# Token mixing of the second and third pair of batches: the first product as seven block products, with sums on GpSimd and shared results in PSUM

## The chip, the cores and the metric

The kernel runs on one core of a Trainium2 chip. The time is the device time of one execution in microseconds. Before the change it is 770.59 us, the median of three runs (770.36 to 770.64).

## What is computed

An attention block without softmax, with 8 batches of 8 heads, 576 rows and a head width of 64, is followed by a mixer. The attention's output, normalised per head, is laid out as x with 576 rows and 512 columns per batch.

```python
kv = np.einsum('bhsd,bhse->bhde', k, v)
out = np.einsum('bhsd,bhde->bhse', q, kv)
rms = np.sqrt(np.mean(out * out, axis=-1, keepdims=True) + 1e-06)
x = out / rms * g_norm                      # then (B, S, H*D)
...
xt = x.transpose(0, 2, 1)
h = np.maximum(xt @ w_tok1, 0.0) @ w_tok2   # 576 -> 256 -> 576
u = x + h.transpose(0, 2, 1)
h2 = np.maximum(u @ w_ch1, 0.0) @ w_ch2     # 512 -> 1536 -> 512
return u + h2
```

The change concerns `xt @ w_tok1`, the first product of token mixing.

## The kernel before

**Tiles and stages.** Batches are handled in four pairs. X of a pair lies in five tiles: four of 128 partitions x 2 x 512 (X[pair, 0] and X[pair, 1] hold the first 512 rows of the pair's first batch, the "side" 0; X[pair, 2] and X[pair, 3] those of side 1), and one of 128 x 512 with the last 64 rows of both batches (X[pair, 4]). Attention of pair p + 1 is interleaved with token mixing of pair p on every engine. When all pairs are done, a channel stage computes the rest from rows that were written to the output in memory and from transposed blocks; it takes most of the time (about 185 us to the end). It is written with seven block products in place of eight already, and so is not touched.

**Order.** The order of work on each engine is written out by hand. `play` (L1317) reads strings of step names and calls each step; every instruction is kept in program order on its engine. The strings `middle` (L1385, mixing of pair 0 and attention of pair 1) and `steady` (L1391, pairs 1 and 2 of the mixing) are the ones that change. A name with "-" belongs to the attention or mixing of the pair before in time, a digit n runs n steps of the weight rounding (clamp L202, shift L206, an addition L211 on DVE, and two scaling activations, L181 and L186 or L196 and L199, on ACT).

**Names.** For a group c of X: a{c} is the attention's product on PE into the PSUM pools o or kv; g{c}{h} multiplies by the gain on DVE (L494); q{c}{h} squares on ACT (L498); t{c}{h} sums the squares on DVE (L522); m, r and i form the inverse of the root mean square (L527 on DVE, L532 on ACT, L536 to L541 on DVE). Then X is scaled: s{c}{t} on ACT (eight activations, L557), d{c}{t} on DVE (L566), p{c}{t} on POOL (L570). kv{s}{h} is the product of k and v on PE and e{s}{h} its copy out on ACT. x{u}{half} are transposes of X on DVE into the unused part of the tile of the second channel weight, and b{u}{half} the DMAs that put them away. f{n} fetches a block of the channel weights, l, lq and lr load k, v and q.

**Token mixing** (`token_mixing`, L598). h{s}{t} (`tok1`, L601) adds four products of 128 x 128 by 128 x 512 into a PSUM bank for side s and half t of the 256 hidden columns; PSUM pool h has four banks. hr (`tok1_rem`, L608) adds the last 64 rows and writes h1 with four Relu activations. z{i} (`seed`, L619) copies a tile of x into a bank ahead of time, so that the second product lands on top of it. u{i} (`tok2`, L625) is the second product: without a seed its result is added to x by DVE, with a seed it is copied back by ACT; every second u, and u8, issues DMAs to the output from the POOL queue. Before the change the seeds are 2, 4 and 6, and the order around the change is: kv00, kv01, u8 and a3 of the neighbouring pairs, h00, h01, a0, h10, h11, hr, a1.

The helpers have one line for all their uses: `tensor_add` L127, `relu` L130, `copy` L133, `matmul` L136, `dma` L124.

Of the kernel before, what the change touches and what calls it, by code (L numbers as in the profile page):

```python
# [11 lines left out]
F32 = mybir.dt.float32  # L12
# [3 lines left out]
ALU = mybir.AluOpType  # L16
# [4 lines left out]
def kernel(  # L21
# [32 lines left out]
    nc = tc.nc  # L54
    P = 128
    B, S, DM = k.shape
# [4 lines left out]
    J, JJ, HF, Q = 4, 5, 64, 32  # L61
    LO = P * J
    assert D == 64 and DM == 512 and S == LO + HF and B % 2 == 0
    NC, NF, NTOK = DM // P, DCH // P, DTOK // P
# [6 lines left out]
    NU = B + 1  # L71
    NG = 1 + B // 2
    T = 2 * P
    assert B // 2 == 4
    EPS = 1e-6
    TOP = (2.0 - 2.0 ** -3 - 2.0 ** -23) * 2.0 ** -96

    def pool(name, bufs, side="left", stack=ctx, **kw):
# [9 lines left out]
    hp_ = pool("hp", 2, "right", right)  # L88
# [7 lines left out]
    ps = {n: pool(f"ps_{n}", b, "left", psums, space=bass.MemoryType.PSUM)  # L96
          for n, b in (("o", 2), ("kv", 2), ("h", 4))}
# [4 lines left out]
    w_tok1 = [tokw.tile([P, 2, DTOK], F32, name=f"w_tok1{i}") for i in range(J // 2)]  # L102
    w_tok1r = tokw.tile([P, DTOK], F32, name="w_tok1r")
# [3 lines left out]
    w_ch2 = w2p.tile([P, 2, NS, 2, DH], F32, name="w_ch2")  # L107
    k_in = [inp.tile([P, JJ, DM], F32, name=f"k_in{i}") for i in range(2)]
# [6 lines left out]
    def do(f, *a, **kw):  # L115
        return lambda: f(*a, **kw)
# [6 lines left out]
    def dma(o, i, engine=nc.sync):  # L123
        keep(engine.dma_start(o, i))  # L124

    def tensor_add(o, a, b, op=ALU.add, engine=nc.vector):
        keep(engine.tensor_tensor(out=o, in0=a, in1=b, op=op))  # L127

    def relu(o, a):
        keep(nc.scalar.activation(o, a, AF.Relu))  # L130

    def copy(o, a):
        keep(nc.scalar.copy(o, a))  # L133

    def matmul(*a, **kw):
        keep(nc.tensor.matmul(*a, **kw))  # L136
# [120 lines left out]
    def get_ch2(f):  # L257

        def loads(raw):
            t = raw.rearrange("p (f n) w -> p f n w", f=2)  # L260
            rows = words(moe_w_ch2)[ts(f, 2 * P)].rearrange("(f p) n w -> f p n w", f=2)
            return [(t[:, i], rows[i]) for i in range(2)]

        dst = w_ch2[:, 2 * f // NS, ds(2 * f % NS, 2)]
        return block(2 * DM, loads, dst.rearrange("p f h n -> p (f h n)"), True)
# [115 lines left out]
    X = {}  # L381

    def x_of(pair, i):

        return X[pair, i // 2][:, i % 2]
# [209 lines left out]
        return steps  # L595


    def token_mixing(pair, seeds, aside=()):  # L598
        h1, acc = {}, {}

        def tok1(side, t, js=range(J)):  # L601
            if js[0] == 0:
                acc[side, t] = ps["h"].tile([P, DM], F32, name="ps_h", tag="h")
            for j in js:
                matmul(acc[side, t], lhsT=w_tok1[j // 2][:, j % 2, ts(t, P)],
                                 rhs=x_of(pair, side * J + j), start=(j == 0), stop=False)

        def tok1_rem():  # L608
            for t in range(NTOK):
                for side in range(2):  # L610
                    r = ds(side * HF, HF)
                    matmul(acc[side, t], lhsT=w_tok1r[r, ts(t, P)],
                                     rhs=x_of(pair, 8)[r], start=False, stop=True)
            for side in range(2):
                h1[side] = hp_.tile([P, NTOK, DM], F32, name="h1", tag="h1")
                for t in range(NTOK):
                    relu(h1[side][:, t], acc[side, t])

        def seed(i):  # L619


            acc[i] = ps["h"].tile([P, DM], F32, name="ps_u", tag="h")
            copy(acc[i], x_of(pair, i))

        def tok2(i):  # L625
            if i not in seeds:
                n = "o" if i in aside else "h"
                acc[i] = ps[n].tile([P, DM], F32, name="ps_u", tag=n)
            first = i not in seeds
            if i < 8:  # L630
                for t in range(NTOK):
                    matmul(acc[i], lhsT=w_tok2[:, t, ts(i % J, P)], rhs=h1[i // J][:, t],
                           start=(first and t == 0), stop=(t == NTOK - 1), skip_group_check=True)
            else:
                for t in range(NTOK):
                    for side in range(2):
                        matmul(acc[i][ds(side * HF, HF)], lhsT=w_tok2[:, t, LO:],
                               rhs=h1[side][:, t],
                               start=(first and t == 0), stop=(t == NTOK - 1), skip_group_check=True)
            x = x_of(pair, i)  # L640
            if first:
                tensor_add(x, acc[i], x)
            else:
                copy(x, acc[i])
            if i == 8:
                dma(u_rest[ts(pair, P)], x, nc.gpsimd)
                for side in range(2):
                    dma(out[2 * pair + side, LO:], x[ds(side * HF, HF)], nc.gpsimd)
            elif i % 2 == 1:
                dma(  # L650
                    u_rows(2 * pair + i // J)[ds((i % J - 1) * P, 2 * P)]
                    .rearrange("(t p) e -> p t e", p=P), X[pair, i // 2], nc.gpsimd)

        steps = {f"h{s}{t}": do(tok1, s, t) for s in range(2) for t in range(NTOK)}
        steps |= {f"h{s}{t}{j}": do(tok1, s, t, (j,)) for s in range(2) for t in range(NTOK) for j in range(J)}
        steps |= {f"z{i}": do(seed, i) for i in seeds}
        return steps | {"hr": tok1_rem} | {f"u{i}": do(tok2, i) for i in range(9)}


    xg, xt, uT = {}, {}, {}  # L660
# [656 lines left out]
    def play(lines, after={}, **stages):  # L1317

        for name in " ".join(lines).split():
            if name.isdigit():
                for _ in range(int(name)):
                    next(stages["rounding"], lambda: None)()
            elif name[0] == "-":
                stages["before"][name[1:]]()
            else:
                next(stages[s][name] for s in ("attention", "mixing", "more")
                     if name in stages.get(s, ()))()
# [3 lines left out]
    tok2 = [get_tok2(t) for t in range(NTOK)]  # L1333
    first_rows = [get_tok1_half(j) for j in range(2)]
    channel = ([get_ch1(c, f) for f in range(2) for c in range(NC)]
               + [get_ch2(f) for f in range(NF // 2)])
    dma(g_row, bass.AP(tensor=g_norm.tensor, offset=g_norm.offset, ap=[[0, 1], list(g_norm.ap[0])]), nc.gpsimd)
    load(0)
    first_rows[0][0]()
# [32 lines left out]
    def spread_g():  # L1372
# [12 lines left out]
    middle = [  # L1385
        "h100 h110 h101 h111 w31 w22 w23 w24", "kv00 e00 -lq1 w32 w33 w34",
        "h102 h112 h103 h113 w41 w42 w43 w44", "kv01 e01", "hr l0 z2",
        "a0 q00 g01 q01 g00 t00 t01", "u0 f0", "u1 z4", "u2", "a1 q10 g11 q11 g10",
        "kv10 kv11 e10 e11 t10 t11 m0 r0 lq0", "u3 z6 i0 d00 s01 d11 f1", "u4 l1", "a2 q20 g21 q21 g20",
        "a4 q40 t20 g41 q41 t21 g40 lr0 lr1", "u5 s10 t40 t41 m2 r2 f2 1", "u6 1 i2 p20 p21 x00", "u7 1 1"]  # L1390
    steady = [[  # L1391
        "kv00 kv01 e00 e01 -d40 f3", "-u8 -a3 -q30 -g31 -q31 -g30 -t30 -t31 -m3 -r3 -lq1",
        "h00 -i3 -d31 -s30 l0 b00 1 1", "h01 f4 x01 1", "a0 q00 g01 q01 g00", "h10 t00 t01 b01 x10 1",
        "h11 1 x11 1", "hr z2 f5 f6", "a1 q10 g11 q11 g10 lq0", "kv10 kv11 e10 e11 t10 t11 m0 r0", "u0 i0 1",
        "u1 z4 d00 s01 l1", "u2", "a2 q20 g21 q21 g20", "a4 q40 t20 g41 q41 t21 g40 lr0 lr1", "u3 z6 d11 1",
        "u4 s10 t40 t41 m2 r2 1 f7", "u5 i2 d20 p21 1 1", "u6 1 f8", "u7 1 1 b10 b11"], [
        "kv00 kv01 e00 e01 -d40 f9", "-u8 -a3 -q30 -g31 -q31 -g30 -t30 -t31 -m3 -r3 -lq1",
        "h00 -i3 -d31 -s30 x20 1", "h01 x21 1", "a0 q00 g01 q01 g00", "h10 t00 t01 1 1", "h11 f10 1 1", "hr z2",
        "a1 q10 g11 q11 g10", "kv10 kv11 e10 e11 t10 t11 m0 r0", "u0 f11 i0 1", "u1 z4 d00 s01", "u2",
        "a2 q20 g21 q21 g20", "a4 q40 t20 g41 q41 t21 g40", "u3 z6 d11 1", "u4 s10 t40 t41 m2 r2 1",  # L1400
        "u5 i2 d20 p21 1", "u6 1 f12 b20 b21", "u7 1", "a3 q30 g31 q31 g30", "u8 t30 t31 m3 r3 f13"]]

    attentions = [attention(0, ((0,), (1,), (2,), (3,), (4,)))]
    attentions += [attention(p, ((0, 1), (2, 4), (3,))) for p in range(1, B // 2)]

    mixings = [token_mixing(p, (2, 4, 6)) for p in range(B // 2 - 1)]
    mixings.append(token_mixing(B // 2 - 1, range(2, 9), (0, 1)))
    more = {f"w{n}{k}": f for n, b in enumerate(first_rows[:1] + tok1[1:] + tok2 + first_rows[1:]) for k, f in enumerate(b)}
    more |= {f"f{n}": b[0] for n, b in enumerate(channel)}
# [11 lines left out]

    more |= {f"j{n}": do(keep_warm, n) for n in (4, 5, 21)}
    more["gs"] = spread_g
    more |= {f"zk{side}{half}": do(spread_k, side, half) for side in range(2) for half in range(2)}
    more |= {f"zz{side}": do(zero_rows, side) for side in range(2)}
    play(start, attention=attentions[0], mixing=mixings[0], more=more)
    play(middle, attention=attentions[1], mixing=mixings[0], before=attentions[0],
         more=more, rounding=rounding)
    for n in range(1, B // 2 - 1):
        play(steady[n - 1], attention=attentions[n + 1], mixing=mixings[n], before=attentions[n] | {"u8": mixings[n - 1]["u8"]},  # L1430
             more=more, rounding=rounding)


# [113 lines left out]
```

## Time and profile before

| | |
|---|---|
| median of the runs | 770.59 us |
| span of the profiled execution | 768.4 us |
| PE busy | 762.0 us, 4694 matmul records |
| DVE busy | 644.5 us |
| ACT busy | 279.5 us |
| POOL busy | 112.8 us |
| first product of token mixing, all four pairs | 128 records of 128 x 512 and 32 of the last rows |
| DMA, mean rate | 245 GB/s |

The span runs from the first to the last instruction of one profiled execution; the run's own time lies 2.2 us above it. The profile lists, for each engine, how long it was busy, and the timeline gives each instruction's start, its length, and in brackets the idle time before it and what ended that. A matmul of single precision leaves two records. PE's records have modelled ends, so starts are used here and not lengths. A group of records that is merged in one line carries the start of its first and the time to the end of its last.

### The profile page before, as it was taken

The numbers are of one execution on the slowest core, as the hardware profiler recorded it, in microseconds if no ns is written. First come the engines' busy times: TensorE is split into PE (matmuls) and PEld (weight loads), VectorE is DVE, ScalarE is ACT, GpSimd is POOL, SyncE is SP. The second block draws the span as 40 slices with busy tenths as digits, with TensorE's granted clock in tenths as the row PEclk, the third lists the DMA queues.
The fourth block names the chain that finished last, engine by engine and source line by source line (L and its number), as shares of the span: only waits on it lengthen the run. The fifth ranks groups of instructions, "written<-read, shape, count | busy, mean of one in ns | idle before, by whom it ended". The sixth has DMA issues, their size and how long they took to land.

```text
span 768.4 us, 12735 instructions
## 1 busy us (share of the span) xinstructions
PE 762.0 (99%) x4694; PEld 614.3 (80%) x4694; DVE 644.5 (84%) x956; ACT 279.5 (36%) x563; POOL 112.8 (15%) x125
## 2 busy tenths in 40 slices
PE   9999999999999999999999999999999999999997
PEld 8655555446888888888888888888888888888887
DVE  4868886997757779899968989997898997798996
ACT  3656666773210332512234241123352213325221
POOL 1003030204410000002240002042000227000204
PEclk9999999999999999999999999999999999999999
DMA  9999997599798795599998578999659889855679
GB/s 353 374 374 371 367 373 279 177 332 333 245 290 319 288 284 169 168 275 214 224 228 250 152 221 219 262 187 265 193 154 293 160 227 209 200 153 155 153 192 119
DMA packets 137981, 188.28 MB, mean 245 GB/s; under 512 B 48704, under 2 KB 95808, under 8 KB 135872
## 3 DMA queue, kind: packets, MB, share of 16 engines
q1 hardware_dynamic: 102240, 168.72, 69.1%
q0 software_dynamic: 34848, 18.36, 16.1%
q8 instruction: 38, 0.62, 0.3%
q10 hardware_dynamic: 832, 0.39, 0.2%
q14 instruction: 23, 0.19, 0.1%
HBM read 138.28 MB, written 49.15 MB: 244 GB/s over the span
## 4 chain that ended last, share of the span: by engine, by line
PE 96%; DMA 2%; DVE 1%; SPq 0%; ACT 0%; issue 0%; DVEq 0%
PE ps_d L136 28%; PE ps_b L136 19%; PE ps_a L136 19%; PE ps_u L136 8%; PE ps_h L136 8%; PE ps_v L136 5%; PE ps_c L136 3%; PE ps_w L136 2%; PE ps_kv L136 2%; PE ps_o L136 2%; DMA raw<-in_moe_w_tok_dram 1%; DMA v_in<-in_k_dram 1%; PE ps_r L136 0%; DVE x L494 0%; DVE ms L522 0%; DVE w_tok L211 0%
## 5 line engine op out<-in xcount | busy, mean ns | idle before, releaser
L136 PE MATMUL ps_d<-ui,w 128*128 128x256 f32 x504 | 118.6, 379 | 0.0
L136 PEld LDWEIGHTS ps_d<-ui,w 128*128 128x128 f32 x504 | 95.8, 190 | 13.0
L133 ACT COPY ps_d<-ps_a 128x768 f32<-128x768 f32 (+1 forms) x56 | 32.0, 572 | 199.9 <-PE ps_a L136 196.9
L127 DVE TENSOR_TENSOR v<-v,v 128x1536 f32<-128x1536 f32 (+2 forms) x70 | 103.2, 1482 | 0.3
L136 PE MATMUL ps_b<-sv,w 128*128 128x256 f32 x324 | 78.9, 379 | 0.0
L136 PE MATMUL ps_a<-v,w 128*128 128x256 f32 x324 | 78.7, 379 | 0.0
L1266 POOL DMA_DIRECT2D out_dram<-us x24 | 26.8, 1835 | 291.8 <-ACT p L133 286.5
L136 PEld LDWEIGHTS ps_b<-sv,w 128*128 128x128 f32 x324 | 61.2, 190 | 8.9 <-issue 0.6
L136 PEld LDWEIGHTS ps_a<-v,w 128*128 128x128 f32 x324 | 61.6, 190 | 8.4
L136 PE MATMUL ps_u<-h,w_tok 128*128 128x512 f32 (+1 forms) x160 | 64.7, 599 | 0.0
L136 PE MATMUL ps_d<-v,w 128*128 128x256 f32 x258 | 62.7, 379 | 0.0
L130 ACT ACTIVATE v<-v 128x768 f32<-128x768 f32 (+1 forms) x54 | 42.6, 822 | 55.1 <-DVE v L127 52.3
L136 PE MATMUL ps_h<-x,w_tok 128*128 128x512 f32 x128 | 57.6, 600 | 0.7 <-DVE w_tok L211 0.6
L1266 POOL DMA_DIRECT2D out_dram<-r x40 | 41.3, 1926 | 102.0 <-ACT p L133 80.3
L136 PE MATMUL ps_d<-sv,w 128*128 128x256 f32 x228 | 55.4, 379 | 0.0
L136 PEld LDWEIGHTS ps_d<-v,w 128*128 128x128 f32 x258 | 48.9, 190 | 6.6
L136 PEld LDWEIGHTS ps_u<-h,w_tok 128*128 128x128 f32 (+1 forms) x160 | 25.6, 179 | 31.1 <-issue 26.7
L136 PEld LDWEIGHTS ps_d<-sv,w 128*128 128x128 f32 x228 | 43.3, 190 | 5.9
L136 PE MATMUL ps_a<-uT,w 128*128 128x256 f32 x192 | 46.7, 379 | 0.0
L136 PEld LDWEIGHTS ps_h<-x,w_tok 128*128 128x128 f32 x128 | 23.5, 190 | 28.3 <-issue 24.4
L136 PE MATMUL ps_b<-ui,w 128*128 128x256 f32 x168 | 40.8, 379 | 0.0
L136 PEld LDWEIGHTS ps_a<-uT,w 128*128 128x128 f32 x192 | 36.5, 190 | 5.0
(178 smaller groups left out, 1297.7 us busy)
## 6 DMA issues: line engine op xcount, KB each, us to landing
w<-parts SPq DMA_DIRECT2D x168, 384.0 KB
w<-parts SPq DMA_DIRECT2D x56, 192.0 KB
uT<-blocks SPq DMA_DIRECT2D x36, 256.0 KB
k_in<-in_k_dram SPq DMA_DIRECT2D x8, 1024.0 KB
v_in<-in_v_dram SPq DMA_DIRECT2D x8, 1024.0 KB
qT<-in_q_dram SPq DMA_DIRECT2D x8, 1024.0 KB
out_dram<-x POOLq DMA_DIRECT2D x16, 512.0 KB, 6.9
raw<-in_moe_w_ch_dram SPq DMA_DIRECT2D x8, 768.0 KB
```

The source lines that it names most:

```text
L127: keep(engine.tensor_tensor(out=o, in0=a, in1=b, op=op))
L130: keep(nc.scalar.activation(o, a, AF.Relu))
L133: keep(nc.scalar.copy(o, a))
L136: keep(nc.tensor.matmul(*a, **kw))
L1266: keep(nc.gpsimd.dma_start(to, t()[ds(b * Q, Q), at].rearrange("p n l j -> p n (l j)"), accum_op=ALU.add))
```

## The change

In the second and third pair (`fast = (1, 2)`), the eight block products of the first product (two halves of the hidden columns, two halves of the rows, two sides; each block product is two matmuls) are replaced by seven, on sums of blocks:

- Four sums of blocks of `w_tok1` (`mix_tok1`, y1 to y4 in `middle`) are formed once on POOL, 128 x 256 each, and kept in a part of the second channel weight's tile that is filled late.
- Four sums of blocks of X (`t_sum`: y1, y2, T1 or T2, and y4 per pair) are formed on POOL, two subtractions of 128 x 512 each. T stands in the line of u5 or u4, in the phase before; y1 and y2 follow u8 on the queue; y4 follows p6.
- The products p1 to p7 run in the order p3, p7, p1, a0, p6, p2, p5, p4 on four banks. Bank a gets p1; ACT copies it to bank e in PSUM, and p6 and p5 are added there; p2 is added to bank a, p7 and p4 share bank d, p3 has bank y. ACT copies out the state of d after p7, and that of e after p6 and after p5.
- hr (`p_rem`) adds the last rows, three additions on DVE join the banks with what was copied out, and three Relu activations write h1.
- Seeds 3 and 5 are added in these pairs (z3, z5), so that u3 and u5 are copied back by ACT.
- The DMAs of u8's rows become a step v8 (`put_rest`) that stands behind y1 and y2 on the POOL queue. The transposes x11 move from h11's place to u0's, and the order of the last blocks of the second channel weight changes.

```diff
+    def tok_sum(n):
+        return weight_room[1].rearrange("p s (g n) -> p (s g) n", n=2 * P)[:, n - 1].rearrange(
+            "p (j n) -> p j n", j=2)
+    def mix_tok1(n):
+        a = lambda m, k: w_tok1[k][:, :, ts(m, P)]
+        x, y, op = {1: (a(1, 0), a(1, 1), ALU.add), 2: (tok_sum(1), a(0, 0), ALU.subtract),
+                    3: (a(0, 0), a(1, 0), ALU.subtract), 4: (a(0, 1), tok_sum(2), ALU.subtract)}[n]
+        tensor_add(tok_sum(n), x, y, op, nc.gpsimd)
...
+        b_block = {11: 2, 12: 0, 21: 3, 22: 1}
+        def t_sum(n):
+            b = lambda name: X[pair, b_block[name]]
+            if n < 3:
+                h1[n - 1] = hp_.tile([P, NTOK, DM], F32, name="h1", tag="h1")
+            txs[n] = h1[0] if n == 1 else h1[1] if n != 3 else spare(pair, 0)
+            x = b({1: 12, 4: 21}.get(n, 22))
+            y = b({1: 11, 3: 12}[n]) if n % 2 else h1[n // 4]
+            for j in range(2):
+                tensor_add(txs[n][:, j], x[:, j], y[:, j], ALU.subtract, nc.gpsimd)
+        def product(name, lhs, rhs, start):
+            if start:
+                bank[name] = ps["h"].tile([P, DM], F32, name="ps_h", tag="h")
+            for j in range(2):
+                matmul(bank[name], lhsT=lhs[:, j], rhs=rhs[:, j], start=(start and j == 0),
+                       stop=False, skip_group_check=True)
+        def p3():
+            product("y", tok_sum(4), x_block(22), True)
+        def p7():
+            product("d", tok_sum(3), txs[3], True)
+            copy(spare(pair, 1)[:, 0], bank["d"])
+        def p1():
+            product("a", a_block(0, 0), x_block(11), True)
+            bank["e"] = ps["h"].tile([P, DM], F32, name="ps_h", tag="h")
+            copy(bank["e"], bank["a"])
+        def p6():
+            product("e", tok_sum(2), txs[2], False)
+            copy(spare(pair, 1)[:, 1], bank["e"])
+        def p2():
+            product("a", a_block(0, 1), x_block(21), False)
+        def p5():
+            product("e", tok_sum(1), txs[1], False)
+            copy(h1[0][:, 0], bank["e"])
+        def p4():
+            product("d", a_block(1, 1), txs[4], False)
+        def p_rem():
...
+            tensor_add(h1[0][:, 0], bank["y"], h1[0][:, 0])
+            tensor_add(h1[0][:, 1], bank["e"], spare(pair, 1)[:, 0])
+            tensor_add(h1[1][:, 1], bank["d"], spare(pair, 1)[:, 1])
+            relu(h1[0], h1[0])
+            relu(h1[1][:, 0], bank["a"])
+            relu(h1[1][:, 1], h1[1][:, 1])
...
-               + [get_ch2(f) for f in range(NF // 2)])
+               + [get_ch2(f) for f in (0, 1, 2, 4, 5, 3)])
...
     steady = [[
-        "kv00 kv01 e00 e01 -d40 f3", "-u8 -a3 -q30 -g31 -q31 -g30 -t30 -t31 -m3 -r3 -lq1",
-        "h00 -i3 -d31 -s30 l0 b00 1 1", "h01 f4 x01 1", "a0 q00 g01 q01 g00", "h10 t00 t01 b01 x10 1",
-        "h11 1 x11 1", "hr z2 f5 f6", "a1 q10 g11 q11 g10 lq0", "kv10 kv11 e10 e11 t10 t11 m0 r0", "u0 i0 1",
...
+        "kv00 kv01 e00 e01 -d40 f3", "-u8 y1 y2 -v8 -a3 -q30 -g31 -q31 -g30 -t30 -t31 -m3 -r3 -lq1",
+        "p3 -i3 -d31 -s30 l0 b00", "p7 1 1", "p1 f4 x01 1", "a0 q00 g01 q01 g00", "p6 y4 t00 t01 b01", "p2 x10 1", "p5 1", "p4 1",
+        "hr z2 z3 f5 f6", "a1 q10 g11 q11 g10 lq0", "kv10 kv11 e10 e11 t10 t11 m0 r0", "u0 x11 i0 1",
...
-    mixings = [token_mixing(p, (2, 4, 6)) for p in range(B // 2 - 1)]
+    mixings = [token_mixing(p, (2, 3, 4, 5, 6) if p in fast else (2, 4, 6)) for p in range(B // 2 - 1)]
```

The third pair's string changes likewise, with one difference that the prediction uses: there "p7 x20 1" and "p1 x21 1" carry one rounding step each, where the second pair has "p7 1 1".

## The prediction

> **What bounds the kernel now.** I read the page first (busy shares, the clock row, the chain that ended last), then the list of waits, then the timeline around the two phases that change, PE first, then ACT, then DVE and POOL.
>
> ```profile
> PE 762.0 (99%) x4694; PEld 614.3 (80%) x4694; DVE 644.5 (84%) x956; ACT 279.5 (36%) x563; POOL 112.8 (15%) x125
> ...
> PEclk9999999999999999999999999999999999999999
> ...
> PE 96%; DMA 2%; DVE 1%; SPq 0%; ACT 0%; issue 0%; DVEq 0%
> ```
>
> PE is busy for 762.0 of 768.4 us, at full clock in every slice, and is 96% of the chain. The list of waits gives PE only two semaphore waits, 1.7 us together, both in the first stage. So a matmul taken out shortens the run by its length, and any new wait of PE lengthens it by the wait: no idle time stands ready to swallow it. This is the second pair's phase on PE:
>
> ```profile
> 69.06 1.16 PE L136 MATMUL ps_o<-kvp,qT 64*64 64x64 f32 x64
> 70.15 7.13 PE L136 MATMUL ps_h<-x,w_tok 128*128 128x512 f32 x16
> 77.21 1.16 PE L136 MATMUL ps_o<-kvp,qT 64*64 64x64 f32 x64
> 78.30 7.13 PE L136 MATMUL ps_h<-x,w_tok 128*128 128x512 f32 x16
> ```
>
> Step a3 starts at 69.06, h00 and h01 at 70.15, a0 at 77.21, h10 and h11 at 78.30. Each matmul leaves two records, so 16 records are 8 matmuls: 77.21 - 70.15 = 7.06 us, 0.88 us each. The third pair shows the same from 111.84.
>
> **What goes.** Sixteen matmuls per pair become fourteen (seven products of two); the instruction lists of the two kernels confirm it. Four fewer at 0.88: **-3.53 us**, all on the path.
>
> **What comes: a wait of PE for ACT.** PE's new order is p3, p7, p1, a0, p6, p2, p5, p4. p6 adds onto bank e, which must first hold p1's result, and an ACT copy brings it there. PE takes its steps in order, so while p6 waits, p2, p5, p4, hr, a1 and all behind them wait too. With p3 at 70.15, PE is ready for p6 at 70.15 + 3 x 1.77 + 1.09 (a0) = 76.54. When is the copy done? ACT is in order as well, and the instruction lists put ahead of it: s30 (eight scalings of X[1,3]), the copy of bank d after p7, and in this pair one rounding step of two activations. ACT in the trace of before:
>
> ```profile
> 75.40 0.21 ACT L532 ACTIVATE root<-ms 128x16 f32<-128x16 f32 x1 [1.33 <-DVE ms L527]
> 76.64 2.02 ACT L557 ACTIVATE x<-x,inv 128x64 f32<-128x64 f32 x8 [1.02 <-DVE inv L541]
> 78.57 0.89 ACT L181 ACTIVATE w_ch<-raw 128x768 f32<-128x768 f32 x1
> 79.37 0.90 ACT L186 ACTIVATE raw<-raw 128x768 uint32<-128x768 uint32 x1
> 80.17 0.57 ACT L498 ACTIVATE sq<-ps_o 128x512 f32<-128x512 f32 x1
> ```
>
> s30 waits until 76.64 for statistics that begin with a3 on PE, which the change leaves where it was. ACT is free of s30 at 78.57; the two rounding activations take 80.17 - 78.57 = 1.60. A copy of 512 columns I take at 0.58 (the rows of ps_u<-x and x<-ps_u have 602 and 576 ns). So p6 cannot start before 78.57 + 0.58 + 1.60 + 0.58 = 81.33: **4.8 us of stall**, where before h10 needed nothing from ACT. In the third pair no rounding stands between:
>
> ```profile
> 111.84 7.13 PE L136 MATMUL ps_h<-x,w_tok 128*128 128x512 f32 x16
> ...
> 116.34 2.02 ACT L557 ACTIVATE x<-x,inv 128x64 f32<-128x64 f32 x8 [1.03 <-DVE inv L541]
> ...
> 118.90 1.16 PE L136 MATMUL ps_o<-kvp,qT 64*64 64x64 f32 x64
> ```
>
> PE is ready at 111.84 + 5.30 + 1.09 = 118.23; ACT at 116.34 + 1.93 + 2 x 0.58 = 119.43: **1.2 us**. These two are floors, as they assume that DVE's statistics come no later than before. Floor of the sum: 4.8 + 1.2 - 3.53 = +2.5 us.
>
> **GpSimd beside DVE.** Each fast pair gets eight POOL subtractions of 512 columns, two (T) before s30's statistics, four (y1, y2) during them, two (y4) behind p6. A POOL operation of 512 has 1245 ns in the mean with waits, and 0.92 to 1.03 without; one of 384 with two full inputs 0.95 to 1.1. I take 1.15. DVE is without idle time from 66.3 to 75.2 (and from 104.8 to 115.1) except for waits on ACT's square root, so what delays DVE delays s30. And POOL does delay it:
>
> ```profile
> 105.97 1.55 POOL L570 TENSOR_TENSOR x<-x,inv 128x512 f32<-128x512 f32 x1
> ...
> 106.52 1.42 DVE L202 TENSOR_SCALAR w_ch<-w_ch 128x768 f32<-128x768 f32 x1
> ...
> 107.98 0.56 DVE L206 TENSOR_SCALAR w_ch<-w_ch 128x768 uint32<-128x768 uint32 x1
> ```
>
> L202 alone takes 0.55; beside a POOL operation that ended at 107.52 it took 1.42, that is, 0.42 past that end. At 147.78 an L211 took 2.08 where its five likes take 1.22 in the mean, again until a POOL operation had ended. If every DVE operation with two inputs in SBUF, the 128x16 ones too, takes turns like this with T, y1 and y2, the inverse that s30 waits for comes 2.7 us later in the second pair: T runs from 65.65 (after s10 and a DMA issue) to 68.4 with L202 between its halves, and holds the two 128x16 operations behind L202 (+1.25); d40 meets y1's first half (some +1.0 more) and L527 the end of y2 (+0.45). In the third pair it is 2.8: ACT's added copy for u3 puts T beside the next inverse (+1.2), p21 comes between L202 and L206 (+0.6), y2 holds L527 (+1.0). If none of this reaches the chain, it is 0. No row shows the small ones beside POOL. I take 1.7 and 1.4, between the ends, nearer the upper in the second pair since T lies right on a 128x768 operation there. Stalls: 6.5 and 2.6 us. The Trainium skill's page "SBUF — State Buffer" (Who interferes with whom) speaks against moving sums to GpSimd here: it calls the shared port pair an exclusive lock for DVE operations in a 2-port mode or with two SBUF inputs. By that rule the delays would be the full 2.7 and 2.8, and the sum below 2.4 us higher.
>
> **The clock.** PE is never idle for long in the trace until its end. There its last matmul ends at 762.25 + 1.50 = 763.75:
>
> ```profile
> 1.07:4.00 2.93, 2.93 (x13) 1.00 0.78 232
> 4.00:6.40 2.40, 2.40 (x13) 1.00 1.00 410
> 6.60:8.40 1.80, 1.80 (x18) 1.00 1.00 386
> ...
> 767.00:767.60 0.60, 0.00 (x0) 1.00 0.00 0
> 767.70:768.40 0.70, 0.00 (x0) 0.50 0.03 12
> ```
>
> The columns are PE's busy time with its records, the clock, DMA. The clock halves some 3.95 us after the last matmul. At the start the same 128-column matmuls pass at 0.18 us a record until about 6.5, then at 0.10: PE, busy from 1.07, took some 5.4 us to get full speed (though the clock's column says 1.00 there). A stall of 6.5 us outlasts 3.95, so the clock should fall in the second pair; 5.4 us at half speed lose up to 2.7 us, none if it holds. I take 2.0. The page "TensorE: Matmul & The Clock Gate" (Part 1) gives windows of about 3.4 us free running, both ways. By it a resumed PE loses 1.7 to 3.4 us, and the sum below would be +7.3 to +9.0.
>
> **What costs nothing.** p7 and p1 wait for POOL's T and p21: done by about 71.3, needed at 71.9 and 73.7. y2 ends near 77.7 and 117.6: before p6 can start anyway, though with only 0.6 to spare in the third pair if ACT were early. p5 needs bank e copied out (0.58), covered by p2's 1.77; p4 needs y4 (2.3), covered by p2 and p5 (3.5). After hr DVE has three additions (0.69) and ACT a Relu of 1024 columns (1.05) ahead of u0; a1 and kv on PE cover 3.57 us, so u0 is late only if DVE is over 1 us late. ACT gains about 4.5 us per pair and sheds no bound; DVE gains three additions and loses two. The seeds z3 and z5 fill banks two products ahead of use. y1, y2 now stand on POOL's queue ahead of the last rows' three DMAs (1.7 us of issue), T ahead of p21 and of one DMA: the rows are read only in later stages, and p21 is needed by p1 alone. The four weight sums (128x256) run in the first pair's phase where POOL idles; the transposes x11 and the order of the last weight blocks only change place on DVE, ahead of a stage that starts after all of them.
>
> **The sum.** 6.5 + 2.6 + 2.0 - 3.53 = +7.6: span 768.4 -> 776.0, and with the 2.2 us by which the median (770.59) lies above the profiled span, **778.2 us**. A difference under 0.2% (1.5 us) can't be told from none.
>
> **The rivals.**
> - *Floor* (0.25): POOL doesn't hold the chain, the clock holds. +2.5 gives 773.1; up to 776. For it: no row shows a small DVE operation held. Against it: DVE has no slack.
> - *Both stalls in full* (0.13): 7.5 + 4.0 and the clock falls twice (2 x 2.7): +13.4, 784.0; from about 781. The third pair's stall would have to pass 3.95 us.
> - *The inputs come in time* (0.06), the other side: bank e is filled before a0 ends, in both pairs, and seven products simply replace eight: -3.53, 767.1. It decides as soon as the two stalls together stay under 3.53 us. For it: ACT is only 36% busy, and DVE sheds additions before the third pair. Against it: s30's place in ACT's list.
> - *Both even out* (0.04): within 0.2%.
> - That the product count doesn't fall is excluded by the instruction lists.
>
> The forecast (stalls with part of the turns, clock falls once; 776 to 781) has 0.52. The range 773.0 to 782.5 takes in the floor and part of the full stalls; it leaves out the two faster or equal cases and the far end, some 0.18. Faster 0.06, same 0.04, slower 0.90.
>
> **What would show it.** The waits of the changed kernel should have PE waiting for ACT's ps_h<-ps_h copy, once over 4.8 us and once over 1.2; ACT's timeline s30, then the copies; the granted clock below 1 in the stretch after the first stall; DVE's operations at 66 to 76 us longer beside POOL. The forecast is wrong if ACT's copy of bank e starts before s30 is done, if a3's statistics finish earlier, or if the clock stays at 1.00 through a stall of over 5 us (then 2 us less).

## The result, and the profile after

The changed kernel takes 796.88 us (median of 4 runs, 794.81 to 797.65) against 770.54 us for the kernel before: a ratio of 1.0339, 95% interval 1.0326 to 1.0351. The prediction was 778.2 us with a range to 782.5, so the side was right and the size far off: +26.3 us instead of +7.6. The profiled execution took 796.38 us, with a span of 794.5.

The page of the changed kernel, in the lines that answer to those of before: the span, the busy row, the clock in 40 slices of 19.9 us, the chain.

```profile
span 794.5 us, 12774 instructions
...
PE 763.3 (96%) x4686; PEld 613.6 (77%) x4686; DVE 661.9 (83%) x958; ACT 286.6 (36%) x577; POOL 135.7 (17%) x145
...
PEclk9999698799999999999999999999999999999999
...
PE 78%; DVE 5%; ACT 5%; SPq 1%; issue 1%; DMA 0%; ACTq 0%; DVEq 0%
```

PE is busy about as long as before (763.3 us against 762.0) and the span is 26 us longer: PE is waiting. The clock falls in two places, slice 5 and slices 7 and 8, which are the second and third pair. The list of PE's waits (total, times, longest):

```profile
PE ps_h L137 <- ACT ps_h L134: 21.8, 2, 11.6
PE ps_u L137 <- ACT h L131: 2.1, 1, 2.1
```

The first is the wait that was predicted, PE for the copy of bank a into bank e on ACT, once in each pair, but of 11.6 and 10.2 us instead of 6.5 and 2.6. The second, 2.1 us in the last pair, was not predicted at all. The second pair's phase on PE (start, length, and in brackets the idle time before):

```profile
70.09 1.98 PE L137 MATMUL ps_h<-x,w_ch 128*128 128x512 f32 x4
71.91 1.88 PE L137 MATMUL ps_h<-w_ch 128*128 128x512 f32 x4
73.63 1.88 PE L137 MATMUL ps_h<-x,w_tok 128*128 128x512 f32 x4
75.44 1.16 PE L137 MATMUL ps_o<-kvp,qT 64*64 64x64 f32 x64
88.17 3.75 PE L137 MATMUL ps_h<-h,w_ch 128*128 128x512 f32 x4 [11.57 <-ACT ps_h L134]
91.71 2.39 PE L137 MATMUL ps_h<-x,w_tok 128*128 128x512 f32 x4
93.94 1.88 PE L137 MATMUL ps_h<-h,w_ch 128*128 128x512 f32 x4
```

p3, p7, p1 and a0 run as planned. p6 starts at 88.17 and not at 81.33 (the floor) or 83.0 (the forecast's 6.5). Then p6 takes 3.54 us to the next start instead of 1.77, and p2 2.23. From the start of this phase to hr 27.38 us pass, where before 15.22 did; in the third pair 26.74. So the two phases cost 12.2 + 11.5 us, and the last pair's wait 2.1: 25.8 of the 26.1 us by which the span grew.

Why was the copy late? The last step of a weight rounding on DVE, a few steps ahead of s30's statistics, before the change:

```profile
70.61 0.96 DVE L211 CUSTOM_DVE_ANT_1 w_ch<-w_ch,raw 128x1536 uint16<-128x1536 uint16 x1
```

ACT, DVE and GpSimd (POOL) in the changed kernel, where this line is L212:

```profile
65.57 2.53 POOL L128 TENSOR_TENSOR w_ch<-x 128x512 f32<-128x512 f32 x2
...
66.25 2.27 DVE L203 TENSOR_SCALAR w_ch<-w_ch 128x768 f32<-128x768 f32 x1 [1.13 <-ACT w_ch L182]
...
72.20 6.24 DVE L212 CUSTOM_DVE_ANT_1 w_ch<-w_ch,raw 128x1536 uint16<-128x1536 uint16 x1
72.68 2.50 POOL L128 TENSOR_TENSOR h<-x 128x512 f32<-128x512 f32 x2
75.13 2.48 POOL L128 TENSOR_TENSOR h<-x,h 128x512 f32<-128x512 f32 x2
...
80.33 0.60 ACT L499 ACTIVATE sq<-ps_o 128x512 f32<-128x512 f32 x1 [9.46 <-DVE x L495]
...
83.50 2.02 ACT L558 ACTIVATE x<-x,inv 128x64 f32<-128x64 f32 x8 [1.02 <-DVE inv L542]
...
87.47 0.59 ACT L134 COPY ps_h<-ps_h 128x512 f32<-128x512 f32 x1
```

This is the whole case in eight rows. L212 takes 6.24 us in place of 0.96, and it ends at 78.44, 0.83 us after the fourth of the subtractions y1 and y2 on GpSimd, which are issued back to back (72.68 to 77.61, 1.25 us each; a burst, from here on). L203, 0.56 us alone, takes 2.27 and ends 0.42 after T. Behind L212 on DVE's list stand the gains of a3, so ACT's second square waits 9.46 us for them; the statistics, their root and s30 follow (83.50, before 76.64), then the copy of bank d, a rounding step, and at 87.47 the copy that p6 waits for. In the third pair it is the 128x512 scaling d40 that the burst catches: 5.83 us, 0.69 alone.

```profile
127.94 5.83 DVE L567 TENSOR_TENSOR x<-x,inv 128x512 f32<-128x512 f32 x1
...
141.31 3.75 PE L137 MATMUL ps_h<-h,w_ch 128*128 128x512 f32 x4 [10.19 <-ACT ps_h L134]
```

There s30 starts 13.64 us after p3, where before it started 4.50 us after h00.

The clock, by stretches (PE's busy time and the granted clock stand in the columns after the stretch and before the DMA share):

```profile
76.50:80.00 3.50, 0.10 (x8) 0.00 (x0) 3.50 (x4) 0.00 (x0) 1.18 (x2) 0.87 1.05 431
80.00:88.00 8.00, 0.00 (x0) 0.00 (x0) 7.51 (x18) 5.31 (x15) 1.61 (x3) 0.50 0.98 366
88.00:92.00 4.00, 3.83 (x5) 1.80 (x6) 3.41 (x9) 1.11 (x4) 1.27 (x1) 0.50 1.02 350
92.00:94.00 2.00, 2.00 (x5) 0.77 (x5) 1.78 (x2) 0.54 (x1) 1.40 (x1) 0.82 0.53 221
```

A mean of 0.87 over 3.5 us is 2.6 us at 1.00 and 0.9 at 0.50: the clock halves at about 79.1, 2.5 us after PE's last matmul, and is back at about 92.7, 4.5 us after PE resumes. In the third pair it halves at about 133.7 (2.6 us after PE stops) and is back at about 147.3, 6 us after PE resumes. p6 and p2 together took 5.77 and 6.50 us instead of 3.53: 5.2 us lost.

### The profile page after: what moved, and what is told of

The parts are those of the page before. It is cut to its first block, busy times and chain, and to the rows that moved or that the text cites. A ratio compares the mean times of both kernels' runs of the same rounds, so it can differ in the third digit from the quotient of the medians.

```text
span 794.5 us, 12774 instructions
## 1 busy us (share of the span) xinstructions
PE 763.3 (96%) x4686; PEld 613.6 (77%) x4686; DVE 661.9 (83%) x958; ACT 286.6 (36%) x577; POOL 135.7 (17%) x145
## 4 chain that ended last, share of the span: by engine, by line
PE 78%; DVE 5%; ACT 5%; SPq 1%; issue 1%; DMA 0%; ACTq 0%; DVEq 0%
PE ps_d L137 27%; PE ps_b L137 18%; PE ps_a L137 18%; PE ps_v L137 5%; PE ps_h L137 3%; PE ps_c L137 3%; PE ps_u L137 2%; PE ps_w L137 2%; ACT x L558 1%; SPq L125 1%; DVE w_ch L212 1%; DVE x L567 1%; DVE ms L523 1%; DVE x L495 1%; ACT ps_u L134 0%
## 5 line engine op out<-in xcount | busy, mean ns | idle before, releaser
L137 PEld LDWEIGHTS ps_u<-h,w_tok 128*128 128x128 f32 (+1 forms) x160 | 25.5, 179 | 34.0 <-issue 26.2
L128 DVE TENSOR_TENSOR v<-ps_b,u 128x768 f32<-128x768 f32 x28 | 26.7, 955 | 15.6 <-PE ps_b L137 12.5
L137 PE MATMUL ps_h<-x,w_tok 128*128 128x512 f32 x80 | 38.3, 624 | 0.7 <-DVE w_tok L212 0.6
```

## The experiments

**Theory** after this: GpSimd's subtractions, issued back to back, hold DVE's operation until the last of them has ended, and not for one of them; what stands behind it on DVE is the chain to s30, and s30 stands before the copies on ACT. **Rivals:** the ACT order alone does it (1), or the statistics are late for another reason, as the added seeds and weight steps (2).

**Without the sums of x (e1).** All eight subtractions of each pair left out; the products read unsummed blocks.

```
-            for j in range(2):
-                tensor_add(txs[n][:, j], x[:, j], y[:, j], ALU.subtract, nc.gpsimd)
+            txs[n] = b({1: 12, 2: 22, 3: 22, 4: 21}[n])
```

> The eight subtractions of X blocks per pair are left out (products p4 to p7 read blocks of X as they are); the weight sums on POOL, the copies, the order and the seeds stay. Theory (POOL's back-to-back subtractions hold DVE, and so the statistics that s30 waits for): DVE's L212 and d40 return to about 0.9 and 0.7 us, s30 starts near 76.6, p6 waits about 5 us in the second pair and 1 to 3 in the third, the clock costs 1 to 2, the block order 2.1: about 777 us (775 to 780). Rival 1 (ACT's longer list alone makes the wait): within 3 us of the changed kernel's 796.9. Rival 2 (p6 waits for the sums themselves): about 769.

Measured: 780.6 us, ratio 1.0137 [1.0113, 1.0161]; 16.3 us less than the changed kernel. L212 takes 0.96 and L203 0.56 us again. DVE and PE in the second pair:

```profile
70.49 0.96 DVE L212 CUSTOM_DVE_ANT_1 w_ch<-w_ch,raw 128x1536 uint16<-128x1536 uint16 x1
...
75.44 1.16 PE L137 MATMUL ps_o<-kvp,qT 64*64 64x64 f32 x64
81.13 3.44 PE L137 MATMUL ps_h<-x,w_ch 128*128 128x512 f32 x4 [4.53 <-ACT ps_h L134]
84.41 1.88 PE L137 MATMUL ps_h<-x,w_tok 128*128 128x512 f32 x4
```

p6 starts at 81.13: the floor of the prediction, 81.33, was right for this pair, and rival 1 falls. In the third pair the wait is 3.3 us, not 1.2: s30 starts 6.8 us after p3 without any subtraction. So the list ahead of it is 2.3 us later than before for another reason, and there rival 2 has a small part. No run separates it, but e1's trace shows where most of it arises: on ACT the squares of a1 start 3.8 us after a1 on PE, where before the change they started 2.1 us after it. Ahead of them stand the Relus, which wait for the three new additions on DVE, and the copy of the added seed. The time is 3.6 us over the 777 that I expected of the theory, and 0.6 over its range. In the profiled execution (779.56) the wait of 3.3 us and 1.5 us of clock after the first stall are part of that; the two longest runs (781.64 and 782.48) were granted a lower mean clock than it, 0.99 instead of 0.998.

**The sums y1 and y2 on DVE (e6).** They are the four that ran beside the statistics; T and y4 stay on GpSimd.

```
-                tensor_add(txs[n][:, j], x[:, j], y[:, j], ALU.subtract, nc.gpsimd)
+                tensor_add(txs[n][:, j], x[:, j], y[:, j], ALU.subtract, nc.vector if n < 3 else nc.gpsimd)
```

> The changed kernel with y1 and y2 of X on DVE (four operations of 0.69 us per pair, ahead of a3's gains) in place of POOL; T, y4 and the weight sums stay on POOL. Theory: DVE works 2.8 us on them where it was held for over 5, so p6 comes about 2.3 us earlier in each pair, and the clock still falls: about 791.5 us (789 to 793.5). Rival (the amount of work is what counts, whichever engine does it first): no earlier than the changed kernel, 796.9.

Measured: 790.52 us, 1.0259 [1.0243, 1.0274]. DVE pays 2.6 us for the four in its own list (1.28 and 1.29 for two each) instead of 5.3 us of hold, and PE's waits for the copy fall from 21.8 to 16.1. Both say that four subtractions beside the statistics cost more than their work.

**The burst alone, in the kernel before (e3, e7).** The kernel before, with four (e3) or two (e7) subtractions into unused room, issued where y1 and y2 stand. No product and no copy is changed. e7 has ((2, 0),) in the loop.

```
+        def burst():
+            room = w_ch2[:, 0, :2].rearrange("p s h n -> p s (h n)")
+            for o, i in ((2, 0), (2, 1)):
+                for j in range(2):
+                    tensor_add(room[:, j], X[pair, o][:, j], X[pair, i][:, j], ALU.subtract, nc.gpsimd)
...
-        "kv00 kv01 e00 e01 -d40 f3", "-u8 -a3 ...
+        "kv00 kv01 e00 e01 -d40 f3", "y -u8 -a3 ...
```

> The kernel before, plus four POOL subtractions of X blocks into unused memory ahead of u8 in the second and third pair, whose results nobody reads. Theory: d40 (or L211) on DVE is held until the burst of 5 us ends, X[1,3] comes some 5 us late, h10's second half waits about 3.3 us in the second pair and 1.5 in the third: about 775.3 us (773.5 to 778). Rival 1 and 2: POOL has idle time there, so 770.5 within 1.

> As the run with the burst in the kernel before, with two POOL subtractions in place of four. Theory (the hold lasts until the burst ends): X[1,3] 2.5 us earlier than with four, the wait of h10 about 1.0 us in the second pair and none in the third: about 771.5 us (770.7 to 773). Rival (a hold ends with the POOL operation that it met, so that the count does not matter): as with four, 777.

Measured: 777.34 us with four (1.0087 [1.0072, 1.0102]), 771.97 us with two (1.002 [1.0011, 1.003]). With four:

```profile
70.69 6.15 DVE L211 CUSTOM_DVE_ANT_1 w_ch<-w_ch,raw 128x1536 uint16<-128x1536 uint16 x1
71.09 4.92 POOL L127 TENSOR_TENSOR w_ch<-x 128x512 f32<-128x512 f32 x4
...
83.98 6.25 PE L136 MATMUL ps_h<-x,w_tok 128*128 128x512 f32 x10 [3.46 <-ACT x L557]
```

With two:

```profile
70.64 3.73 DVE L211 CUSTOM_DVE_ANT_1 w_ch<-w_ch,raw 128x1536 uint16<-128x1536 uint16 x1
71.04 2.50 POOL L127 TENSOR_TENSOR w_ch<-x 128x512 f32<-128x512 f32 x2
```

The same operation takes 6.15 us beside four, 3.73 beside two and 0.96 beside none (70.61 in the kernel before): two subtractions more, 2.42 us more. It ends 0.83 us after the burst both times. So GpSimd work that nothing reads costs this kernel 7 us (with four: 5.1 us of waits on PE, and a stretch of 3.4 us at half clock), and the hold lasts for the burst. That rules out the rival of e7, by which the count does not matter. The mechanism is shown apart from the change.

**The copies ahead of s30 (e2).**

```
-        "p3 -i3 -d31 -s30 l0 b00", "p7 1 1", "p1 f4 x01 1", "a0 ...
+        "p3 -i3 -d31 l0 b00", "p7", "p1 -s30 1 1 f4 x01 1", "a0 ...
```

> Full computation; ACT gets the copies of banks d and e ahead of s30 (and ahead of the second pair's rounding activations), but still behind the square root of a3's statistics. Theory (DVE is late, so the square root is): copies near 82.5 and 137.2 by the changed kernel's clock, p6 some 4.5 and 2.8 us earlier than in the changed kernel, p2 then near its own limit by s30: about 789 us (786 to 792). Rival 1 (the place of the copies behind s30 is the whole cost): about 771.

Measured: 791.38 us, 1.0273 [1.0258, 1.0288]. p6 starts at 83.65 instead of 88.17: s30 and the rounding step no longer stand before the copies. But a3's second square and the root do, and they wait for the held DVE. The order on ACT is worth 5.5 us and isn't the main cause.

**The last weight blocks in their old order (e4).**

```
-               + [get_ch2(f) for f in (0, 1, 2, 4, 5, 3)])
+               + [get_ch2(f) for f in range(NF // 2)])
```

> The changed kernel with the weight blocks of the second channel weight in the order of before (0 to 5). Theory: ACT's scaling of a block no longer waits for the DMAs that put the transposes away, so the last pair's Relu is on time and the 2.1 us wait of u0 there goes: about 794.8 us. Rival (that wait belongs to something else): 796.9.

Measured: 793.74 us, 1.0305 [1.0289, 1.032]; the wait of 2.1 us before u0 of the last pair is gone from the list. In the changed kernel ACT's scaling there waits for the DMAs that put the transposes away:

```profile
188.03 1.25 ACT L197 ACTIVATE w_ch<-raw 128x512 f32<-128x512 f32 x2 [4.98 <-DMA blocks<-w_ch]
...
192.86 2.04 ACT L131 ACTIVATE h<-ps_h 128x512 f32<-128x512 f32 x4
```

A new order of the blocks has a block written into room that still holds transposes; the Relus for u0 stand behind that wait.

**Can the product scheme win? (e5, e9, e8, e10, e11, e12)** All six compute everything; they differ in order and in which engine does small work. e5 has the old block order, T behind the GpSimd scaling p21, and no rounding step and no d40 on DVE between the statistics of X[1,2] and s30; p1 goes first, so that bank e is copied before a3's root.

```
-        "kv00 kv01 e00 e01 -d40 f3", "-u8 y1 y2 -v8 -a3 -q30 -g31 -q31 -g30 ...
-        "p3 -i3 -d31 -s30 l0 b00", "p7 1 1", "p1 f4 x01 1", "a0 ...
+        "kv00 kv01 e00 e01 f3", "-u8 y1 y2 -v8 -a3 -q30 -g31 -q31 p1 -g30 ...
+        "p3 -i3 -d31 -s30 -d40 l0 b00", "p7 1 1", "1 f4 x01 1", "a0 ...
```

> Full computation, all seven products and all sums on POOL. The weight blocks in the order of before; T behind p21 on POOL; no rounding step and no d40 on DVE between i2's statistics and s30 (they follow s30); p1 first on PE, and its copy to bank e ahead of the square root on ACT. Theory (only DVE's large two-input operations are held, and ACT's order did the rest): s30 near its place before, p6 waits under 1 us for y2 in each pair, the clock holds: 770.3 - 3.5 + 1 to 2.5 = about 768.5 us (767.5 to 771). Rival (POOL's sums hold the 128x16 operations and the gains as well): stalls of 3 us and more, 774 or above.

Measured: 787.05 us, 1.0213 [1.0198, 1.0228]: missed. p6 waits for nothing now. The gains (one input in PSUM) and the reductions run beside the burst at their usual length. But then:

```profile
72.77 3.99 DVE L528 TENSOR_SCALAR ms<-ms 128x16 f32<-128x16 f32 x1
```

A 128x16 operation (0.17 us alone) is held until 76.76; the burst ends at 76.71. So the rival has it for the 128x16 operation, and not for the gains. And p5 now waits for a copy that stands on ACT behind a square, which waits for a gain behind the rounding steps that I had moved (3.9 us in the second pair, 5.9 in the third). With each of these two stalls the clock falls to half, at 86.1 for 3.4 us and at 133.9 for 6.8.

e9 takes this mean to ACT (the first part of the diff) and changes nothing else. e8 has both parts: p6's copy stands ahead of the squares, the rounding steps behind the gains and in the token mixing.

```
             ms = stat[g][0]
+            if pair and g == (3,):
+                keep(nc.scalar.activation(ms, ms, AF.Copy, scale=1.0 / D, bias=EPS))
+                return
...
-        "p3 -i3 -d31 -s30 -d40 l0 b00", "p7 1 1", "1 f4 x01 1", "a0 q00 g01 q01 g00", "p6 y4 t00 t01 b01", "p2 x10 1", "p5 1", "p4 1",
+        "p3 -i3 -d31 -s30 -d40 l0 b00", "p7", "a0", "p6 y4 q00 g01 q01 g00 t00 t01 x01 b01", "p2 1", "p5 1", "p4 1 f4",
```

> The kernel of e5 with one change: the mean of the third group's statistics (a 128x16 tensor_scalar, held for 3.99 and 3.38 us beside GpSimd's burst in e5) is computed by ACT. Theory (GpSimd's back-to-back subtractions hold the DVE operations of the chain before s30): the chain no longer stops there. The 128x16 scalar_tensor_tensors that follow may still be held by one subtraction each (1.25 us), so s30 starts at 75 to 77.5 instead of 78.03, PE's waits for s30's x (2.6 us in e5) go, the waits for the copy of bank e behind sq01 (5.9 and 3.9 us) stay or change little: 783 to 786 us. Rival 1: the hold passes on to the next DVE operation in the chain, whatever it is, until the burst has ended; then s30 starts at 77.5 or later and the time is that of e5, 787.0 within 1 us. Rival 2: the statistics were never what e5 loses by; the same 787.

> As e9, and in both pairs p6 with its copy of bank e is put ahead of the next squares on ACT, and the rounding steps and transposes behind the gains of that stage (later in the token mixing), so that no copy of PSUM stands on ACT behind a square that waits for DVE. Full computation. Theory: both kinds of waits that were left in e5 go (2.6 + 9.8 us of its 14.3), the clock stays at 1.00, small waits of 1 to 4 us stay: 768 to 774 us; 768 or less would beat the kernel before. Rival (the hold passes on to the next DVE operation): s30 only at 77.5 or later, p2 waits 1.5 to 3 us per pair for it: 774 to 779. Rival 2 (the rounding steps moved behind hr make the h additions late, u0 waits for ACT's Relus): waits PE ps_u <- ACT h of over 2 us per pair, 774 to 780.

Measured: e9 783.47 us, 1.017 [1.0153, 1.0187]; e8 783.27 us, 1.0159 [1.0142, 1.0175]. In e9 the time fits the theory, but s30 starts at 77.38, next to what rival 1 says, since the hold passed on to the next small operation:

```profile
73.66 3.19 DVE L541 SCALAR_TENSOR_TENSOR ms<-ms,inv 128x16 f32<-128x16 f32 x1
74.33 2.48 POOL L128 TENSOR_TENSOR h<-x,h 128x512 f32<-128x512 f32 x2
```

e8 missed its 768 to 774, and its rivals' ranges as well. The copies behind squares are gone, yet the steps that I moved into the token mixing keep DVE full there, and PE waits for the seeds of ps_u:

```profile
PE ps_u L137 <- ACT ps_u L134: 10.2, 2, 6.2
```

e10 spreads these steps over the stretches in which DVE has room.

```
-        "p6 y4 q00 g01 q01 g00 t00 t01 x01 b01", "p2 1", "p5 1", "p4 1 f4",
+        "p6 y4 q00 g01 q01 g00 1 t00 t01 x01 b01", "p2 1 f4", "p5 1", "p4",
...
-        "u4 s10 t40 t41 m2 r2 1 1 f7", "u5 i2 d20 p21 T2", "u6", "u7 b10 b11"]
+        "u4 s10 t40 t41 m2 r2 1 f6", "u5 i2 d20 p21 T2 x20 1", "u6 x21 1", "u7 1 f7 b10 b11"]
```

> The kernel of e8 with another place for DVE's list alone: in e8 PE waited twice for the ACT copy that seeds bank ps_u (4.0 and 6.2 us, with the clock falling after the second), because the rounding steps and transposes that had been moved into the token mixing kept DVE full there (13.6 of 14 us between 96 and 110) and a square on ACT ahead of the seed waited for DVE's gain. Here some of these steps go one stage forward (beside the gains) and some into the stretch between 110 and 120, where DVE was idle (3.8 of 10 us busy). Full computation. Theory (what is left in e8 is only DVE's list in the token mixing): these waits fall under 2 us together, the clock stays at 1.00, small waits of 1 to 3 us remain: 768 to 772 us. Rival (the sheer sum of DVE's work between a3's statistics and the next is too much beside GpSimd's holds, wherever it is put): waits of over 3 us turn up at another place, h or ps_h or ps_u behind ACT, 773 to 782.

Measured: 777.15 us, 1.0086 [1.007, 1.0103]. The theory's range (768 to 772) is missed, and the time lies in its rival's; but what is left are smaller waits, 8.2 us together at six places and none over 2.5, where the rival had waits of over 3. The burst still holds the small operation, to its end at 77.00:

```profile
73.55 3.48 DVE L541 SCALAR_TENSOR_TENSOR ms<-ms,inv 128x16 f32<-128x16 f32 x1
```

e11 sets the issue of one output DMA (w8, u_rest<-x, taken out of v8) between y1 and y2 on GpSimd's queue, seeds u6 one product earlier and takes some rounding steps forward.

```
-        "kv00 kv01 e00 e01 f3", "-u8 y1 y2 -v8 -a3 -q30 ...
+        "kv00 kv01 e00 e01 f3", "-u8 y1 -w8 y2 -v8 -a3 -q30 ...
...
-        "u1 z4 d00 s01 x10 l1 1", "u2 z5", ...
+        "u1 z4 d00 s01 x10 l1 1", "u2 z5 z6", ...
```

> The kernel of e10 with three edits of order. (1) On GpSimd's queue the issue of one output DMA (0.6 us) stands between the two pairs of subtractions y1 and y2, so that the burst of four (5.0 us) becomes two bursts of two (2.5 us each). Theory (DVE gets its turn when GpSimd pauses, not between back-to-back subtractions): the 128x16 scalar_tensor_tensor that was held 3.48 us in e10, to the end of the burst at 77.0, ends at about 74.6, s30 starts at about 75.5 to 76.0 instead of 77.57, and PE's waits for s30's x (1.2 and 1.5 us) go; y2 ends some 0.6 us later, which costs p6 0.5 us at most. Rival: a pause as short as a DMA issue is not enough, the operation is held to the end of y2 as before, s30 at 77.5 or later. (2) The seed of u6 one product earlier on ACT: the waits for ACT's ps_u (1.7 and 1.2 us) go. (3) Some rounding steps earlier, so that ACT's scalings no longer stand before the last pair's squares: the wait of 2.45 us goes. Full computation. All three: 769 to 773 us; with the rival on (1): 771.5 to 775.

Measured: 773.81 us, 1.0046 [1.0029, 1.0062]; 0.8 us over its range. First DVE, then GpSimd, in the second pair (PE is 1.3 us later there than in e10):

```profile
74.84 0.75 DVE L541 SCALAR_TENSOR_TENSOR ms<-ms,inv 128x16 f32<-128x16 f32 x1
75.62 1.19 DVE L543 SCALAR_TENSOR_TENSOR root<-root,ms 128x16 f32<-128x16 f32 x1
```

```profile
72.39 2.50 POOL L128 TENSOR_TENSOR h<-x 128x512 f32<-128x512 f32 x2
74.83 0.59 POOL L125 DMA_DIRECT2D u_rest<-x  x1
75.44 2.50 POOL L128 TENSOR_TENSOR h<-x,h 128x512 f32<-128x512 f32 x2
```

A pause of 0.6 us is enough: the operation that took 3.48 us in e10 takes 0.75 and ends at 75.59, 0.15 us after y2 has begun. In e11 it came only 0.05 us before the first two subtractions ended; e12, which has the same pause, shows it for one that came in their midst. There L541 starts at 73.79, the subtractions end at 74.66, the DMA issue takes the time until 75.18, and L541 ends at 75.35. PE's waits for s30 in these two pairs are gone, those for the seeds down to 0.4.

e12 moves the transposes, one scaling and two rounding steps once more, to get rid of the waits that were left.

```
-        "u4 s10 t40 t41 m2 r2 1", "u5 i2 d20 p21 T2 x20 1", "u6 x21 1 f7", "u7 1 b10 b11"]
+        "u4 s10 t40 t41 m2 r2 1 x20", "u5 i2 d20 p21 T2 1", "u6 1 f7", "u7 x21 1 b10 b11"]
...
-        "u5 i2 d20 p21 1 f12", "u6 1 b20 b21", "u7 1"
+        "u5 i2 d20 d21 1 f12", "u6 b20 b21", "u7"
...
-        "h00 -i3 -d31 -s30 2 -d40 2 o0"
+        "h00 -i3 -d31 -s30 2 -d40 2 2 o0"
```

> The kernel of e11 with its last waits taken up by order alone: the transposes before the third pair one stage earlier and one later, so that DVE's addition that frees a bank for p7 isn't late (p7 waited 0.6 us, p6 for GpSimd 0.8); the scaling before the last pair on DVE instead of GpSimd (a rounding step beside it took 1.87 instead of 0.69 us), and two rounding steps behind the last pair's s30 (PE waited 1.6 us for it). Full computation. Theory: these waits (3.0 us of 773.8) go: 770 to 772, so that the changed order of products stands level with the kernel before; what is left against 767.1 is then the small waits (0.4 to 0.7 us each) and the gap of 0.7 us before ps_r. Rival: the moved steps make another wait of about the same size, 772.5 to 775.

Measured: 775.65 us (5 runs), 1.0069 [1.0055, 1.0083]: worse than e11, as its rival said, and 0.65 us over the rival's range too. The transpose x21 now stands ahead of a rounding step on DVE, and so the step meets the burst. DVE in the third pair, where y1 runs from 115.39 to 117.88, and the new wait on PE's list:

```profile
113.99 1.41 DVE L783 STREAM_TRANSPOSE w_ch<-x 128x256 f32<-128x256 f32 x4
115.33 2.97 DVE L203 TENSOR_SCALAR w_ch<-w_ch 128x768 f32<-128x768 f32 x1
118.22 0.68 DVE L128 TENSOR_TENSOR x<-ps_u,x 128x512 f32<-128x512 f32 x1
```

```profile
PE ps_h L137 <- DVE x L128: 3.4, 2, 2.9
```

L203 begins 0.06 us before y1 and is held until y1 is over; behind it DVE's addition for u8 is late, which frees a bank, and p7 waits 2.9 us for that bank. The case again in small, made by a transpose of 1.4 us at the wrong place.

No version beat the kernel before. e11 is the best, 3.5 us above it: with its order 22.8 of the 26.3 us come back. The 3.5 us of the four matmuls are more than eaten by new waits of 0.3 to 1.6 us at eight places (5.4 us together) and by smaller delays that I did not trace. Whether an order without them exists is open.

## Why the prediction was wrong

- **The four matmuls, -3.53:** right. In e11, where the phase has no wait in the second pair, it takes 13.50 us from its start to hr, 1.72 less than before.
- **PE waits for ACT's copy behind s30:** right as a mechanism; the floor of the second pair was 81.33 and e1 gave 81.13. The third pair's floor was 1.2 and e1 gave 3.3: under "What costs nothing" I had asked whether the additions and the Relu behind hr make u0 late, and not whether the squares behind them on ACT come late.
- **GpSimd holds DVE, +1.7 and +1.4: this step failed.** Measured: s30 is late by 6.9 us in the second pair and by 9.1 in the third, of which 2.3 stay without the subtractions (e1); so they cost it 6.9 and 6.8. Even the upper ends, 2.7 and 2.8, were too low, so this is not a choice inside the range. The row that I priced it from (L202 at 1.42 us, one POOL operation beside it) was read as a turn: a DVE operation waits for one POOL operation, then goes. The rows that I used show a DVE operation held by one POOL operation, and none that meets the boundary between two, so they could not show that the turn often doesn't come there. I also split the delay over the small operations of the statistics (the two behind L202 are 128x24, not 128x16) and gave d40 one half of y1, while it was one large operation ahead of a3's gains that met the whole burst. The weighing of the page "SBUF — State Buffer" (Who interferes with whom) went wrong at the same place: I took its exclusive lock as at most one GpSimd instruction per DVE operation. The page states that whoever issues first has the ports for its whole instruction; here L212 starts at 72.20, before the first subtraction at 72.68, and is still held until after the fourth. But GpSimd was issuing a DMA from 71.92 to 72.66, so the trace does not tell which of the two had the ports first.
- **The clock falls once, 2.0:** it fell twice, for 5.2 us. Longer stalls explain the second time. The time until it falls was wrong too: I took 3.95 us after the last matmul, from the end of the kernel, and no fixed time fits the runs. The clock halved 2.5 and 2.6 us after PE's last matmul here, 4.1 in e1's first stall, and 2.1 in a stall of only 2.45 us in e10, while a stall of 3.3 us in e1 left it at 1.00. What all traces share is how long it stays at half: 13.65 us twice here (79.1 to 92.7 and 133.7 to 147.3), 3.41 in e1, e3 and e10, 6.8 in e5, 10.24 twice in e6, always a multiple of 3.41 us. The page "TensorE: Matmul & The Clock Gate" (Part 1) speaks of free-running windows of about 3.4 us, and these lengths agree. A window need not be wholly idle for the clock to fall: in the 3.41 us before 79.1 PE had worked for 0.9. The estimate from that page in the prediction, 1.7 to 3.4 us for a fall, holds for both falls (2.2 and 3.0).
- **"What costs nothing":** the order of the last weight blocks, of which I said that it only changes place on DVE, cost the wait of 2.1 us in the last pair. e4 is 3.1 us faster, but in its profile one stretch at half clock is also 3.4 us shorter, which need not come from the order. I had looked at DVE's list and not at who last used the room that a block is written to.
- **Rivals:** "both stalls in full" (784.0) was the nearest, and its terms were the right ones, with the wrong bound.

By terms: stalls 11.57 + 10.19 instead of 9.1, clock 5.2 instead of 2.0, last pair 2.1 instead of 0, less 3.53: 25.5 of the 26.1 us by which the span grew; the other 0.6 lies in small delays.

## What to carry to other kernels

Work that is moved to GpSimd in back-to-back operations beside a DVE that is on the path is to be priced by the length of the whole burst, put on the first DVE operation that it catches (a large one in the changed kernel, one of 128x16 in e5), with everything behind that on DVE. Look at what DVE does in that stretch before moving anything there, and if it must be there, break the burst (a DMA issue of 0.6 us was enough). An engine that is 99% busy gains nothing from fewer instructions if they make it wait for an engine whose list holds a serial chain; 3.5 us of matmuls were bought with 21.8 us of waiting for one copy here.

## What the runs showed of the hardware

- Held by a burst of GpSimd subtractions: rounding steps, 128x512 scalings, and small ones down to a 128x16 tensor_scalar (3.99 instead of 0.17 us) and a 128x16 scalar_tensor_tensor (3.48). Not held: gains with one input in PSUM, reductions, transposes and the 128x16 reciprocal (0.25 us in the burst of e9). A held operation ended 0.03 us (128x16, e10) to 0.83 us (L212) after the last subtraction.
- A turn between two back-to-back subtractions does come at times: in the third pair of the changed kernel a 128x24 operation got in after one (0.92 us), and in e11 a 128x16 one (1.19). In e9 and e10 such operations missed every boundary until the end. What decides it the runs don't tell.
- GpSimd pays as well where DVE does get in: T took 2.5 us in the changed kernel, where it held DVE's operations, and 3.52 in e12 beside two rounding steps of DVE that took 1.42 and 1.91.
- The clock halved 2.5 and 2.6 us after PE's last matmul in the stalls of the changed kernel, 4.1 after it in e1, 2.1 in e10, and 3.95 at the end of the kernel before; in e3 it halved at 84.76, 0.8 us after PE had resumed. It stayed at half for multiples of 3.41 us. PE worked for 3.0 us (e1), 4.5 and 6 us (the changed kernel) before it came back.
